# A retention block and a SwiGLU block on one core: the first head pair by chunks of 128 tokens, products of the identity around the first transposes, and another order of the first loads

## The chip, the cores and the metric

The kernel runs on one core of a Trainium2 chip. The metric is the device time of one execution in microseconds (us), the median of several runs. A core has five engines with a queue of instructions each: TensorE (PE in the profile; PEld is its weight load), VectorE (DVE), ScalarE (ACT), GpSimd (POOL) and SyncE (SP). Transfers (DMA) are issued from the queues of SP, ScalarE and POOL. Each engine works its own queue in order.

## The reference

```python
# q, k, v: batch 8, heads 8, 576 tokens, head size 64, float32
scores = (1 / sqrt(64)) * q @ k.T
gamma = 1 - 2 ** (-5 - arange(H))                 # one decay per head
Dmat = where(i >= j, gamma ** (i - j), 0)
attn = (scores * Dmat) @ v                        # causal, no softmax
x = attn.transpose(0, 2, 1, 3).reshape(4608, 512)
g = x @ w_gate                                    # 512 x 1536, float64 in memory
out = (g * sigmoid(g) * (x @ w_val)) @ w_out      # w_out: 1536 x 512
```

## The kernel before

*Two stages that overlap.* Retention makes `x`; the second stage turns tiles of `x` into rows of the result. Tile 0 has 512 tokens (`T0`) and is done with plain products (`up0`, `down0`); the later ones have 1024 and use fewer products of sums and differences (lines 1186 and 1381, most of PE's time). An order written out by hand fixes each engine's queue.

*Pairs.* The 64 head and batch combinations are worked in pairs of heads; pair `i` is batch `i // 4`, heads `2p` and `2p + 1`. Pairs 0 to 3 (`i < HP`) give tile 0 and have a path of their own. A pair is cut into chunks of 64 tokens (`L`). Its steps:
- `load(i)`: q, k and v, 128 KB a transfer for pairs 0 to 3. For pairs 1 to 3 q comes in another order, is scaled by POOL (`scale_run`, line 735) and then transposed. `kn` is k, token by token; `v` likewise.
- `transposes(i)`: PE turns q and k of 4 x 128 tokens by the identity (line 466); copies put them into `qT` and `kT`. Then k is scaled for the states (`keys`, line 505 or 507).
- `scores(i)`: 16 products of 64 x 64 (line 573), two PE instructions each, within a chunk. `new_states(i)`: what each chunk adds to the state (line 543). `masked(i)`: the decay mask `near` (line 580), then the running states: `copies` (584), `pairs` (596), `odd` (603), `evens` (608).
- `own_values(i)` (line 532) and `earlier_values(i)` (line 559) sum the output in `outer`; `to_x(i)` puts it into `x` (line 640, a copy for pairs 1 to 3; line 645 for pair 0, which still has to be scaled by `qry`).

*Weights.* They are float64 in memory and come in 18 blocks of 1024 KB: block 0 is 256 columns of the gate, block 1 the same of val, 2 and 3 the next 256, 4 and 5 those after them; the list `order` mixes the later ones with blocks of `w_out`. `load_w(m)` fetches block m: 0 to 3 in transfers of 256 KB on SP, 0 and 1 half by half, block 4 on SP, block 5 and later on ScalarE's queue. Three raw places are used in turn, so block m + 3 or m + 4 is fetched when block m has been split; block 3 goes to `x_odd`. `split(j)` (lines 389 and 390, ScalarE) and `rounding(j)` (406 and 407, VectorE) make float32 of half block j; `rounding(j)` calls `split(j + 1)` unless told not to. The order of halves is: block 0 and block 1, first halves; their second halves; then both halves of block 2, of block 3, and so on.

*Tile 0's products.* `up0(f, chunks)` (line 853, or 850 for some) makes 128 columns of gate and val from `x` of the pairs in `chunks`: one product for each pair. After the last pair ScalarE takes the Silu (856) and VectorE multiplies (857). `up0(f)` uses banks A and B for even f, C and E for odd f, so `up0(f + 2)` waits for that Silu and that product. `up0(0)` and `up0(1)` need the halves of blocks 0 and 1; `up0(2)` and `up0(3)` those of 2 and 3.

*The order at the start.* `tick(t, 0, HP)` runs for t = 0 to 5: transposes of pair t, scores and states of pair t - 1, values of pair t - 2. In t = 3 come `split(0)`, `rounding(0)`, after it `load(4)` and `rounding(1)`; in t = 4 `up0(0)` for the first two pairs, pair 3, the fetch of block 5 (`held`), `split(4)` and `up0(1)` for two pairs; in t = 5 pair 3's values and `rounding(4)`, `rounding(5)`. Then `up0(0)` and `up0(1)` for pairs 2 and 3, `load(5)`, and a list `plan` in which `rounding(6)`, pair 4's tick, `rounding(7)` to `rounding(9)`, `up0(2)`, `up0(3)` and so on follow.

*The queues of the first loads.* SP: 64 columns of the table `tab`, half of pairs 0 and 1, `load(2)`, the rest of the table (line 337), `load(3)`, then the weight blocks 0 to 3, `load(4)`, block 4, `load(5)`. ScalarE: the other half of pairs 0 and 1 with the values of pair 1, then the Silu of line 316, which loads a table.

## Time and profile before

| | |
|---|---|
| runs | 1017.63, 1017.77, 1018.7 us; median 1017.77 |
| profiled execution | 1019.25 us; its span, first to last instruction, 1017.5 us |
| busy in the span | PE 1001.9 us, DVE 713.2, POOL 564.4, ACT 285.5 |
| PE busy in 0 to 5, 5 to 10, 10 to 15, 15 to 20, 20 to 25, 25 to 30 us | 0.58, 3.94, 4.28, 4.73, 3.75, 4.73 us |
| PE busy in 55 to 60, 125 to 130 us | 3.88, 3.75 us |
| read and written | 194.38 MB, mean 191 GB/s; 251 GB/s in the first 80 us |

The page gives for each engine the busy time and, below, the busy share in 40 slices of the span (a digit is tenths). A line of the timeline has the start and the length of a group of like instructions, the engine, the line of the kernel, the operation with the tile it writes and those it reads, the number of instructions and, in brackets, how long the engine stood idle before and what ended that. A product of float32 operands is two PE instructions. Lines of "SPq" and "ACTq" are DMA issues on those queues. A line of the waits has the waiting engine and line, what ended the wait, the sum in us, how often, and the longest. A line of the windows has a stretch, its length, then busy us (and instructions) of PE, PEld, DVE, ACT and POOL, the granted clock, the DMA engines' busy share and GB/s.

### The profile page before, as it was taken

The numbers are of one execution on the slowest core, as the hardware profiler recorded it, in microseconds if no ns is written. First come the engines' busy times: TensorE is split into PE (matmuls) and PEld (weight loads), VectorE is DVE, ScalarE is ACT, GpSimd is POOL, SyncE is SP. The second block draws the span as 40 slices with busy tenths as digits, with TensorE's granted clock in tenths as the row PEclk, the third lists the DMA queues.
The fourth block names the chain that finished last, engine by engine and source line by source line (L and its number), as shares of the span: only waits on it lengthen the run. The fifth ranks groups of instructions, "written<-read, shape, count | busy, mean of one in ns | idle before, by whom it ended". The sixth has DMA issues, their size and how long they took to land.

```text
span 1017.5 us, 21317 instructions
## 1 busy us (share of the span) xinstructions
PE 1001.9 (98%) x8336; PEld 825.5 (81%) x8336; DVE 713.2 (70%) x1203; ACT 285.5 (28%) x636; POOL 564.4 (55%) x591
## 2 busy tenths in 40 slices
PE   6999999999999999999999999999999999999998
PEld 5644455888888888888888888888888888888887
DVE  4478889678785765967768678866575767566644
ACT  4465622132423312133322101233320012232110
POOL 3400339979575318575565248756672586566515
PEclk9999999999999999999999999999999999999999
DMA  9999887777587887657677777434454554445653
GB/s 241 253 253 241 218 241 253 203 236 218 126 252 192 232 205 215 191 167 197 184 202 204 183 186 202 165 127 165 165 176 142 149 192 146 144 155 181 185 156 100
DMA packets 278892, 194.38 MB, mean 191 GB/s; under 512 B 212552, under 2 KB 246088, under 8 KB 278792
## 3 DMA queue, kind: packets, MB, share of 16 engines
q1 hardware_dynamic: 251464, 94.70, 36.5%
q10 hardware_dynamic: 26688, 97.92, 29.1%
q8 instruction: 66, 1.08, 0.5%
q0 software_dynamic: 640, 0.39, 0.2%
q14 instruction: 34, 0.28, 0.1%
HBM read 154.04 MB, written 38.93 MB: 190 GB/s over the span
## 4 chain that ended last, share of the span: by engine, by line
PE 83%; DMA 5%; DVE 4%; SPq 3%; ACT 2%; POOL 2%; issue 1%; ACTq 1%; DVEq 0%; POOLq 0%
PE bankB L1186 11%; PE bankC L1186 11%; PE bankA L1186 11%; PE bankE L1186 11%; PE bankB L1381 7%; PE bankC L1381 7%; PE bankE L1381 6%; PE bankA L1381 6%; PE inner L1186 2%; PE outer L1186 2%; DMA qk<-in_q_dram 1%; POOL rest L1042 1%; PE outer L532 1%; PE outer L559 1%; PE inner L573 1%
## 5 line engine op out<-in xcount | busy, mean ns | idle before, releaser
L1042 POOL TENSOR_TENSOR rest<-rest 128x512 f32<-128x512 f32 (+1 forms) x141 | 150.3, 1077 | 160.8 <-DVE rest L1042 113.2
L1201 POOL TENSOR_TENSOR arena<-rest,io 128x256 f32<-128x256 f32 x168 | 123.8, 748 | 90.9 <-ACT io L1200 86.3
L1200 ACT ACTIVATE io<-rest 128x256 f32<-128x256 f32 x192 | 79.1, 417 | 202.1 <-DVE rest L1042 134.1
L1186 PE MATMUL bankB<-rest,arena 128*128 128x256 f32 x448 | 114.7, 380 | 0.1
L1042 DVE TENSOR_TENSOR rest<-bankB,rest 128x512 f32<-128x512 f32 x116 | 78.6, 686 | 42.0 <-PE bankB L1186 29.5
L1186 PE MATMUL bankC<-rest,arena 128*128 128x256 f32 x416 | 106.4, 380 | 0.1
L1186 PE MATMUL bankA<-rest,arena 128*128 128x256 f32 x412 | 104.8, 379 | 0.0
L1042 DVE TENSOR_TENSOR rest<-bankC,rest 128x512 f32<-128x512 f32 x110 | 74.6, 685 | 39.3 <-PE bankC L1186 25.3
L1042 DVE TENSOR_TENSOR rest<-bankA,rest 128x512 f32<-128x512 f32 x110 | 74.6, 686 | 37.5 <-PE bankA L1186 18.9
L1042 DVE TENSOR_TENSOR rest<-bankE,rest 128x512 f32<-128x512 f32 x106 | 71.9, 685 | 36.8 <-PE bankE L1186 17.6
L1186 PE MATMUL bankE<-rest,arena 128*128 128x256 f32 x372 | 94.9, 380 | 0.6 <-DVE rest L1042 0.6
L1186 PEld LDWEIGHTS bankB<-rest,arena 128*128 128x128 f32 x448 | 84.6, 190 | 12.5 <-DVE rest L1042 0.7
L1186 PEld LDWEIGHTS bankC<-rest,arena 128*128 128x128 f32 x416 | 78.5, 190 | 11.9 <-DVE rest L1042 1.3
L1186 PEld LDWEIGHTS bankA<-rest,arena 128*128 128x128 f32 x412 | 78.1, 190 | 10.9 <-DVE rest L1042 0.2
L1186 PEld LDWEIGHTS bankE<-rest,arena 128*128 128x128 f32 x372 | 70.3, 190 | 10.7 <-DVE rest L1042 1.2
L1042 POOL TENSOR_TENSOR arena<-arena 128x256 f32<-128x256 f32 (+1 forms) x76 | 70.0, 943 | 9.0 <-PE bankC L1186 7.6
L886 POOL TENSOR_TENSOR rest<-rest 128x512 f32<-128x512 f32 x21 | 29.1, 1408 | 77.5 <-DVE rest L407 60.5
L1381 PE MATMUL bankB<-arena 128*128 128x256 f32 x264 | 61.0, 381 | 0.0
L1381 PE MATMUL bankE<-arena 128*128 128x256 f32 x264 | 60.8, 380 | 0.0
L1381 PEld LDWEIGHTS bankE<-arena 128*128 128x128 f32 x264 | 50.0, 190 | 6.9
L1381 PEld LDWEIGHTS bankB<-arena 128*128 128x128 f32 x264 | 49.8, 190 | 6.9
L1381 PE MATMUL bankA<-arena 128*128 128x256 f32 x240 | 55.3, 380 | 0.0
(267 smaller groups left out, 1879.0 us busy)
## 6 DMA issues: line engine op xcount, KB each, us to landing
arena<-up ACTq DMA_DIRECT2D x63, 896.0 KB, 4.7
arena<-dn ACTq DMA_DIRECT2D x65, 384.0 KB, 3.1
arena<-dn SPq DMA_DIRECT2D x39, 384.0 KB, 3.3
out_dram<-rest SPq DMA_DIRECT2D x31, 256.0 KB, 3.4
qk<-in_q_dram SPq DMA_DIRECT2D x108, 72.0 KB, 3.2
qk<-in_k_dram SPq DMA_DIRECT2D x108, 72.0 KB, 3.3
dn<-rest SPq DMA_DIRECT2D x26, 256.0 KB, 3.0
up<-arena SPq DMA_DIRECT2D x13, 512.0 KB, 5.8
```

What stands on the lines that cost most here:

```text
L532: m = nc.tensor.matmul(value(i, hl, c), s["v"][rows, at], ret[rows, c % 2 if whole(i) else hl, c // 2], start=start, stop=start, skip_grou ...
L559: nc.tensor.matmul(xr[half[hl]] if c + 1 == NC else value(i, hl, c), state[half[hl], c, :], s["qT"][half[hl], ts(c, L)], start=False, stop ...
L573: nc.tensor.matmul(sc[chunk(i, hl, 2 * c + r)[0], r if whole(i) else hl, c], kT[half[hl], at], qT[half[hl], at], start=True, stop=True, sk ...
L886: eng.tensor_tensor(out=dst, in0=srcs[0], in1=srcs[1], op=ALU.add if op[0] == "add" else ALU.subtract)
L1042: eng.tensor_tensor(out=out, in0=a, in1=b, op=ALU.add if sign > 0 else ALU.subtract)
L1186: m = nc.tensor.matmul(b[:, g * TB : (g + 1) * TB], w[:, g], x, start=(opens and g == 0), stop=True, skip_group_check=True)
L1200: nc.scalar.activation(out=s, in_=src[:, 0:TB], func=AF.Silu)
L1201: (nc.vector if busy and o != 2 and qd + 1 < NQ else nc.gpsimd).tensor_tensor(out=hid[:, qd, 2 * H + h, 2 * T + t], in0=src[:, TB : 2 * TB ...
L1381: nc.tensor.matmul(b[:, m * TB : (m + 1) * TB], lhs[:, qd, ts(m, P)], w[:, qd], start=(opens and qd == 0 and m == 0), stop=(qd == NQ - 1), ...
```

## The change

Pair 0 is worked by chunks of 128 tokens with functions of its own. `first_scores` transposes q and k with products of the identity with itself into bankB before (six), between (two) and after (one) them; nobody reads those. VectorE scales q while it takes it from the bank (`first_qry`), so the output of pair 0 needs no scaling any more and ScalarE copies it (`first_out`). Scores are 128 x 128, with a mask of their own (`first_near`); `first_states` makes four states instead of eight. The table gets 132 columns more, all in its first part.

The loads move: q and k of pair 0, then the table's first part, q and k of pair 1, then v of both (v of pair 1 behind the Silu on ScalarE), `load(2)`. `load(3)` comes after the first halves of blocks 0 and 1, the rest of the table after block 2. The order of pairs 0 to 3 is written out, with `up0(0)` in pieces between the pairs (`parts` picks gate or val). From `for c in range(2, HP)` on the order is as before. Lines that only rename or drop code for pair 0 in `transposes`, `masked` and `tick` are left out below.

```diff
-             both(g[:, None] ** L), both(g[:, None] ** (2 * L)), pieces, runs, both(scale * g[:, None] ** at),
+             both(g[:, None] ** L), both(g[:, None] ** (2 * L)), pieces, runs, g[:2] ** -lane, g[:2] ** (2 * L - lane),
+             np.repeat(scale * g[:2, None] ** np.arange(2 * L), L, axis=0), both(scale * g[:, None] ** at),
...
-            for h in heads:
-                queues[i % 2].dma_start(out=blocks(t)[:, h % 2], in_=v[b, h, 0:CW].rearrange("(c p) d -> p c d", p=P))
+                if i == 0 and queue is nc.sync:
+                    nc.sync.dma_start(out=tab[:, 0:NCOL], in_=decays[:, 0:NCOL])
+            def values():
+                for h in heads:
+                    queues[i % 2].dma_start(out=blocks(t)[:, h % 2], in_=v[b, h, 0:CW].rearrange("(c p) d -> p c d", p=P))
+            loaded[i] = (qk, kn, t)
+            return values
...
-    NCOL = 6 * H + 4 * HP
-    nc.sync.dma_start(out=tab[:, 0:NCOL], in_=decays[:, 0:NCOL])
-    load(0)
-    load(1)
+    NCOL = 6 * H + 4 * HP + 4 + P
+    values = [load(0), load(1)]
     ident = const.tile([P, P], F32, name="ident")
     make_identity(nc, ident)
     nc.scalar.activation(out=io[:, 0:1], in_=ident[:, 0:1], func=AF.Silu)
+    for f in values:
+        f()
+    load(2)()
...
+    first_inv, first_key, first_qry = tab[:, NCOL - P - 4 : NCOL - P - 2], tab[:, NCOL - P - 2 : NCOL - P], tab[:, NCOL - P : NCOL]
...
+    first_near, first_ret = arena[:, 2048:2304], arena[:, 1024:2048].rearrange("p (h c i) -> p h c i", h=2, i=P)
+    nc.gpsimd.affine_select(out=first_near.rearrange("p (h i) -> p h i", i=P), in_=first_inv.unsqueeze(2).to_broadcast([P, 2, P]),
+                            compare_op=ALU.is_ge, fill=0.0, base=0, channel_multiplier=-1, pattern=[[0, 2], [1, P]])
...
-    load(2)
-    nc.sync.dma_start(out=tab[:, NCOL:], in_=decays[:, NCOL:])
-    load(3)
...
-    for f in range(2):
-        for m in range(2):
-            load_w(m, (f,))
+    for m in range(2):
+        load_w(m, (0,))
+    load(3)()
+    for m in range(2):
+        load_w(m, (1,))
     load_w(2)
+    nc.sync.dma_start(out=tab[:, NCOL:], in_=decays[:, NCOL:])
     load_w(3)
...
+            for n, (t, src, bank) in enumerate(((kT, kn, bankC), (qT, qk, bankE))):
                 for c in range(NFULL):
-                    to = bank[:, c : 4 * P : NFULL] if t is qT and scaled(i) else bank[:, ts(c, P)]
-                    nc.tensor.transpose(to, src[:, ts(c, P)], ident)
-
-            def put(t, _, bank):
-                if i or t is qT:
-                    copy(t[:, 0:CW], bank)
-                else:
-                    copy(t[:, 0 : CW // 2], bank[:, 0 : CW // 2])
-                    nc.scalar.copy(t[:, CW // 2 : CW], bank[:, CW // 2 :])
-
-            if i + 1 == HP:
-                for part in parts:
-                    turn(*part)
-                pieces = [lambda part=part: put(*part) for part in parts]
-            else:
-                for part in parts:
-                    turn(*part)
-                    put(*part)
+                    nc.tensor.transpose(bank[:, c : 4 * P : NFULL] if n else bank[:, ts(c, P)], src[:, ts(c, P)], ident)
+                pieces.append(lambda t=t, bank=bank: nc.scalar.copy(t[:, 0:CW], bank))
...
-        return [keys] + pieces
+        return pieces + [keys] if i < HP else [keys] + pieces
...
+    first = [(c, hl) for c in range(NFULL) for hl in range(2)]
+    head = lambda c, hl: slice((2 * c + hl) * D, (2 * c + hl + 1) * D)
+    sums = bankA[:, 0 : NFULL * D].rearrange("p (c d) -> p c d", d=D)
+    def first_scores():
+        qk, kn, vt = loaded.pop(0)
+        qT = early[0]
+        st[0] = dict(qT=qT, kn=kn, v=vt)
+        for src, bank, idle in ((None, None, 6), (qk, bankE, 2), (kn, bankC, 1)):
+            for c in range(NFULL if bank else 0):
+                nc.tensor.transpose(bank[:, ts(c, P)], src[:, ts(c, P)], ident)
+            for _ in range(idle):
+                nc.tensor.matmul(bankB[:, 0:P], ident, ident, start=True, stop=True)
+        blocks = lambda a: a.rearrange("p (c i) -> p c i", i=P)
+        table = lambda a: a.unsqueeze(1).to_broadcast([P, NFULL, P])
+        nc.vector.tensor_tensor(out=blocks(qT), in0=blocks(bankE), in1=table(first_qry), op=ALU.mult)
+        nc.vector.tensor_copy(kT[:, 0 : CW // 2], bankC[:, 0 : CW // 2])
+        nc.scalar.copy(kT[:, CW // 2 : CW], bankC[:, CW // 2 :])
+        for hl in range(2):
+            at = kn[:, 0:CW].rearrange("p (g d) -> p g d", d=D)[:, hl::2]
+            nc.vector.tensor_scalar(out=at, in0=at, scalar1=first_key[:, hl : hl + 1], scalar2=None, op0=ALU.mult)
+        for c, hl in first:
+            nc.tensor.matmul(inner[:, hl, ts(c, P)], kT[half[hl], ts(c, P)], qT[half[hl], ts(c, P)],
+                             start=True, stop=True, skip_group_check=True)
+        for hl in range(2):
+            nc.vector.tensor_tensor(out=first_ret[:, hl], in0=blocks(inner[:, hl]), in1=table(first_near[:, ts(hl, P)]), op=ALU.mult)
+    def first_states():
+        s = st[0]
+        for c, hl in first:
+            nc.tensor.matmul(sums[half[hl], c], s["kn"][:, head(c, hl)], s["v"][:, head(c, hl)],
+                             start=True, stop=True, skip_group_check=True)
+        nc.vector.tensor_copy(state[:, 1], sums[:, 0])
+        for c in range(1, NFULL):
+            nc.vector.scalar_tensor_tensor(out=state[:, c + 1] if c + 1 < NFULL else end_states[:, 0], in0=state[:, c],
+                                           scalar=step[:, HP : HP + 1], in1=sums[:, c], op0=ALU.mult, op1=ALU.add)
+    def first_own():
+        for c, hl in first:
+            st[0]["own"] = nc.tensor.matmul(outer[half[hl], 0, ts(c, P)], st[0]["v"][:, head(c, hl)], first_ret[:, hl, c],
+                                            start=(c == 0), stop=(c == 0), skip_group_check=True)
+    def first_out():
+        s = st.pop(0)
+        wait = nc.tensor.nop()
+        tc.add_manual_dep(wait.ins, s["own"].ins.name,
+                          mybir.DependencyInfo(mybir.DependencyClass.Sync, mybir.DependencyReason.DATA), reason="row halves")
+        for c, hl in first[2:]:
+            nc.tensor.matmul(outer[half[hl], 0, ts(c, P)], state[half[hl], c], s["qT"][half[hl], ts(c, P)],
+                             start=False, stop=True, skip_group_check=True)
+        nc.scalar.copy(out=xs[0][:, 0], in_=outer[:, 0])
+    def new_pair(i):
+        scores(i, True)
+        new_states(i)
+        pieces.extend(masked(i))
+        go_on(3)
+    def turn_pair(i):
+        for f in transposes(i):
+            f()
...
-    def up0(f, chunks):
+    def up0(f, chunks, parts=range(2)):
 
         pair = banks[2 * (f % 2) : 2 * (f % 2) + 2]
-        for gv, bank in enumerate(pair):
+        for gv in parts:
+            bank = pair[gv]
             for c in chunks:
...
-    for t in range(HP + 2):
-        tick(t, 0, HP)
-
-        if t == 3:
-            load(HP)
-        for j in {3: (1,), 5: (4, 5)}.get(t, ()):
-            rounding(j)
+    scale_run(1)
+    first_scores()
+    scale_run(2)
+    turn_pair(1)
+    first_states()
+    first_own()
+    new_pair(1)
+    turn_pair(2)
+    first_out()
+    split(0)
+    rounding(0, False)
+    scale_run(3)
+    new_pair(2)
+    own_values(1)
+    split(1)
+    up0(0, [0], [0])
+    earlier_values(1)
+    to_x(1)[0]()
+    put = transposes(3)
+    rounding(1, False)
+    for f in put:
+        f()
+    load(HP)
+    up0(0, [1], [0])
+    up0(0, [0], [1])
+    split(2)
+    own_values(2)
+    earlier_values(2)
+    up0(0, [1], [1])
+    to_x(2)[0]()
+    rounding(2)
+    rounding(3, False)
+    new_pair(3)
+    while held:
+        held.pop()()
+    split(4)
+    up0(1, range(2))
+    own_values(3)
+    earlier_values(3)
+    to_x(3)[0]()
+    for j in (4, 5):
+        rounding(j)
```

## The prediction

> **What bounds the kernel now.** I read the page first: PE 1001.9 of 1017.5 us, so nearly every PE gap and every slow PE stretch is paid, and the change can only act through them. The waits then say where the 15.6 us of gaps lie. From 58 us to the end the largest is 1.3 us, at 127 us; all the rest that matters is in the first 58 us, which is where the change works.
>
> ```profile
> PE   6999999999999999999999999999999999999998
> PE bankE L864 <- DVE arena L857: 1.3, 1, 1.3
> PE bankA L853 <- ACT io L856: 1.1, 1, 1.1
> ```
>
> Second, the timeline of the start. The same four transposes or 32 small products take some 0.6 of the time from 16 us on, with no other change:
>
> ```profile
> 5.87 1.09 PE L466 MATMUL bankB<-ident,kn 128*128 128x128 f32 x4 [0.36 <-DMA kn<-in_k_dram]
> 12.33 1.13 PE L573 MATMUL inner<-rest,kT 64*64 64x64 f32 x32 [0.72 <-ACT rest L470]
> 15.10 1.11 PE L466 MATMUL bankB<-ident,rest 128*128 128x128 f32 x4
> 16.01 0.64 PE L466 MATMUL bankA<-ident,rest 128*128 128x128 f32 x4
> 17.43 0.69 PE L573 MATMUL inner<-rest,kT 64*64 64x64 f32 x32 [0.17 <-ACT rest L470]
> ```
>
> (The granted-clock column says 1.00 throughout; only durations show it.) From the start of L573 to the start of its successor it is 0.81 us at 7.47 and 0.46 at 17.43: a ratio of 1.76. PE became fast after its first stretch without a gap, 12.33 to about 15.9 us. Third, the timeline from 24 to 58 us:
>
> ```profile
> 30.87 1.88 PE L853 MATMUL bankE<-rest,arena 128*128 128x512 f32 x4
> 30.97 0.44 ACTq L370 DMA_DIRECT2D rest<-in_moe_w_val_dram  x1
> 43.95 0.81 SPq L370 DMA_DIRECT2D rest<-in_moe_w_gate_dram  x1
> 52.80 0.67 ACT L389 ACTIVATE rest<-rest 128x512 f32<-128x512 f32 x1 [6.18 <-DMA rest<-in_moe_w_gate_dram]
> 56.77 0.59 ACT L856 ACTIVATE io<-bankA 128x512 f32<-128x512 f32 x1
> 57.41 3.70 PE L853 MATMUL bankA<-rest,arena 128*128 128x512 f32 x8 [1.12 <-ACT io L856]
> ```
>
> Here PE, which has been continuous since 34 us, stops at 56.29 and resumes at 57.41. It waits for `up0(2)`'s Silu to free bankA. That Silu stands on ScalarE behind `split`s of weight block 4, and ScalarE stood idle 6.18 us until that block (1024 KB, issued by SP at 43.95) landed at 52.70. So block 4 at 52.70 + 4.71 us fixes the start of `up0(4)`, however early PE comes to it. Last, windows of 1 us: how full the DMA engines are before that landing (last two columns: share, GB/s).
>
> ```profile
> 25.00:26.00 1.00, 1.00 (x4) 0.39 (x3) 0.56 (x2) 1.00 (x3) 0.00 (x0) 1.00 0.94 260
> 28.00:29.00 1.00, 0.73 (x37) 0.57 (x28) 0.69 (x1) 0.01 (x1) 0.00 (x0) 1.00 0.69 200
> 29.00:30.00 1.00, 1.00 (x8) 0.49 (x3) 0.42 (x1) 0.37 (x1) 0.00 (x0) 1.00 0.61 161
> ```
>
> From 2 us on they are full; 28 to 30 us is the largest hole.
>
> **Part 1: the start, up to the end of `up0(1, range(2))`.** Before, that ends at 32.75 us.
>
> *Identity products.* Each is two PE instructions of 128 columns. A 256-column instruction takes 0.216 us (L1186, 8 in 1.73 us), so 128 columns take 0.108, or 0.19 while slow (by 1.76): nine cost 1.9 to 3.4 us. Six fill the idle time between the identity (ready at 1.50) and the first q (4.42 before); six by 0.38 slow end at 3.8. Two (0.76) meet the 0.36 us wait for k, one (0.38) the 0.52 us wait for `kT`. If PE stays slow they overrun by about 0.4 us.
>
> *Scores of pair 0.* The 32 instructions of 64x64 (0.69 fast, 1.13 slow) become 16 of 128 columns on half the rows. No row has that shape: below, half of 0.69 is 0.35; above, 16 x 0.108 = 1.7 one after another; I take pairs side by side as the small ones run, 0.86 fast and 1.5 slow. States stay near 0.4, own values grow by the same 0.4, earlier values to some 0.6. Together PE gets 0 to 2 us more, I take 1.1.
>
> *VectorE.* q's scaling takes the copy's place (0.69 for 0.69). The mask becomes two of 0.69, one more; against it `pairs` (0.47) and `evens` (0.48) fall away for a 64-column copy (0.2), and the three L645 outputs (1.30) move to one ScalarE copy of 0.59. About 1 us less. POOL gets one `affine_select` more (128x256; two of 64x512 take 1.37), before `scale_run(1)` and under the wait for q of pair 1.
>
> *Transfers.* The table's part needed first grows from 64 to 196 columns, all of it by 132: 0.068 MB. Landings fit a line: k of pair 1 (1.60 MB issued up to it) at 9.64, `x_odd` (7.63 MB) at 30.89, so 3.52 us a MB. `load(3)` (0.79 MB) and the table's remainder (0.26) now stand behind weight halves: the first halves of blocks 0 and 1 land near 16.4 for 19.8 us, pair 3's v at 19.1 (16.1), the second halves at 22.8 (23.5), blocks 2 and 3 at 26.5 and 31.1 (27.2, 30.89). Queued behind the later pair 3 on SP are only those halves. Values of pair 1 now stand behind the Silu on ScalarE (table load 1.28), harmless: they are first read near 12 us.
>
> *Sum.* PE's work is spread over transfers, so the last transfer sets the end: second halves 22.8 + `split` 1.23 (ScalarE, 21.23 to 22.46) + rounding 1.26 (VectorE, 22.02 to 23.28) = 25.3, + 1.88 for the val half of `up0(1)` = 27.2 us, against 32.75: **5.5 us ahead**. Pair 0's shape, the filled gaps and the faster clock lie under the transfers.
>
> **Part 2: from there to `up0(4)`.** Own and earlier values of pair 3 and 16 products follow (32.68 to 41.14). Half of the products need pair 3's copies, which stand on ScalarE behind the issue of block 5 (30.97 before, just after `x_odd` landed at 30.89) and one `split`; that can give back up to 1.7 us. `up0(2)` thus starts at 35.7 to 37.4. Its 13.9 us with `up0(3)` end at 49.6 to 51.3 (the last quarter needs VectorE's rounding that ended at 46.82; it wants it at 46.1 to 47.8). With 1.3 us of pair 4, PE stands before `up0(4)` at 50.9 to 52.6, 3.7 to 5.4 us earlier. The wait of 1.12 us becomes 4.8 to 6.5: the stall is moved, not removed, unless block 4 lands earlier.
>
> **Part 3: block 4's landing.** The same megabytes go ahead of it (pairs 0 to 4, blocks 0 to 3, and on ScalarE's queue 5 and 6) plus 0.068 MB: +0.24 us. Block 5 may now be issued while `x_odd` is still moving and fill the hole of 28 to 30 us: shares 0.69 and 0.61 against 1.06 (mean of 23 to 28) lack 0.8 us; I take 0.7. Bounds: nothing is filled, +0.24; everything under 1.06 from 28 to 52 us is filled, 2.8, so -2.5 us. [...]
>
> **Part 4: after `up0(4)`.** ScalarE's splits and the later weight loads hang on the same landing, so VectorE's late product at 127 us moves with it. Total: +0.24 - 0.7 = **-0.5 us**. The profiled execution (1019.25 us, span 1017.5) becomes 1018.75; it lies 1.48 us over the median of 1017.77, so I predict 1017.3.
>
> **Rivals.**
> A, *block 4 comes much earlier*. Blocks 5 and 6 (30.97 and 36.58 before) are issued up to 5 us earlier, and two busy queues move more: in 5 to 12 us, with both, shares are 1.17 to 1.36. That over 28 to 52 us would give the 2.5 us of the bound, or up to the 5.4 us PE is ahead: 1012.4 to 1015.3, about 1014.8. Against: 43 to 52 us holds little but block 4 itself.
> B, *the clock falls back in the longer wait* before `up0(4)`. No wait in this trace after 16 us exceeds 1.3 us, so nothing shows it; for it speaks that the start stayed slow until 15.9 us, though PE had worked 11.5 us with gaps of 0.2 to 0.7. It decides if the wait passes the length the clock tolerates. Price: the one gapless slow stretch lasted 3.5 us, and by the ratio 1.76 that loses 1.5; 11.5 us would lose 5.0. With -0.5 that is +1.0 to +4.5, from 1018.8 to 1022.3, some of it hidden by the 1.3 us at 127. [...]
> C, *SP is blocked ahead of block 4*. One SP issue of v stood 7.9 us until a w_out block of ScalarE's queue landed:
>
> ```profile
> SPq L287 <- DMA rest<-in_moe_w_out_dram: 7.9, 1, 7.9
> ```
>
> If block 5, issued earlier, comes to hold up pair 4's loads so, block 4 is issued late. Block 5 needs some 8 us; what moves meanwhile is one queue's at half the rate, so 2 to 4 us are lost: 1020 to 1021.5. Against: before 44 us SP never waited over 1.4 us.
> D, *the products don't raise the clock* (transposes lie between). Pairs 0 and 1 then cost PE what they cost before (7.47 to 15.1 us hold 7 us, 3 of them by the slow rate); PE is at most those 3 us less ahead, still ahead of block 4: 1017.5.
>
> **Chances.** Forecast 0.36 and D 0.02: within 0.2% (2 us, about what a measurement of this kernel tells from no change). A 0.26: faster. B 0.20: 0.07 within, 0.13 slower. C 0.16: slower. So faster 0.26, same 0.45, slower 0.29. The forecast's own range is 1015.3 to 1018.5; with most of A, B and C it is 1013.7 to 1020.9.
>
> **What will show it.** Right: transposes and products at the fast durations before 10 us; `up0(1)`'s val half done near 27 us; ScalarE's long wait for block 4 again ending at 52 to 53; PE's wait before `up0(4)` at 4 to 6 us. Wrong: block 4 landing under 50 us (A); L853 of 128x512 at 0.76 us each instead of 0.43 after that wait (B); an SP wait of several us between 29 and 44 (C); slow transposes after 10 us (D). A `up0(4)` that starts by more than 2 us off 57 us breaks the forecast.

## The result, and the profile after

The changed kernel takes 1022.64 us (median of 6 runs, 1021.35 to 1026.0) against 1017.7 for the one before in the same session: a ratio of 1.0062, 95% interval 1.0049 to 1.0075. It is slower by 4.9 us; 1017.3 was forecast, with a range of 1015.3 to 1018.5. The profiled execution took 1022.28 us, its span is 1020.6 us (1017.5 before).

The page of the changed kernel: busy time with the number of PE instructions (46 products and 46 loads fewer than the 8336 before, which is 23 products of the program, each two loads and two products), the busy shares of PE, and the queue that brings the instructions themselves.

```profile
PE 1005.3 (99%) x8290; PEld 828.6 (81%) x8290; DVE 708.8 (69%) x1200; ACT 286.8 (28%) x636; POOL 564.4 (55%) x592
...
PE   8989999999999999999999999999999999999998
...
q8 instruction: 66, 1.08, 0.4%
```

PE is busy 3.4 us *longer* than before although it has fewer instructions: some of them ran slowly. The list of PE's waits has the rest; the columns are the sum, how often, and the longest.

```profile
PE bankA L868 <- ACT io L871: 2.9, 1, 2.9
PE inner L559 <- issue: 2.0, 1, 2.0
PE bankA L879 <- issue: 1.6, 1, 1.6
...
PE bankA L868 <- DVE arena L416: 1.3, 1, 1.3
```

The first is the wait ahead of `up0(4)`, 1.1 us before. The second and the third were not there before. "Issue" means that PE waited for nothing that the profile shows. (All lines of the changed kernel lie 15 further down from `up0` on: 868 and 871 are 853 and 856 of before, 398 and 416 are 389 and 407, 559 and 529 are 573 and 543, 518 and 545 are 532 and 559.)

The start, in the timeline of PE: the transposes run at the fast rate from the second four on, and the val half of `up0(1)` for two pairs (the L868 into bankE) ends at 30.1 us.

```profile
4.28 1.06 PE L734 MATMUL bankE<-ident,qk 128*128 128x128 f32 x4
5.75 0.60 PE L734 MATMUL bankC<-ident,kn 128*128 128x128 f32 x4
28.26 1.88 PE L868 MATMUL bankE<-rest,arena 128*128 128x512 f32 x4
```

The place where the forecast ended, ScalarE's and PE's timelines merged: block 4 lands, its `split`s, the Silu, then `up0(4)`.

```profile
51.92 0.66 ACT L398 ACTIVATE rest<-rest 128x512 f32<-128x512 f32 x1 [3.28 <-DMA rest<-in_moe_w_gate_dram]
53.06 0.64 PE L559 MATMUL inner<-qT,kT 64*64 64x64 f32 x30
55.93 0.58 ACT L871 ACTIVATE io<-bankA 128x512 f32<-128x512 f32 x1
56.57 5.40 PE L868 MATMUL bankA<-rest,arena 128*128 128x512 f32 x8 [2.87 <-ACT io L871]
61.80 2.74 PE L868 MATMUL bankB<-rest,arena 128*128 128x512 f32 x6
```

`up0(4)` starts 0.84 us earlier than before, but its gate half takes 5.40 us instead of 3.70, so its val half starts 0.85 us *later* (61.80 for 60.95). Windows show why (the clock fell at 56.69 and at 623.30 us; the bounds lie 0.05 us behind that); after the stretch and its length come busy us (and instructions) of PE, PEld, DVE, ACT and POOL, then the granted clock.

```profile
49.90:53.30 3.40, 3.40 (x63) 1.69 (x63) 0.52 (x2) 1.38 (x3) 0.00 (x0) 1.00 1.15 202
53.30:56.74 3.44, 0.57 (x27) 0.44 (x20) 1.82 (x4) 2.93 (x6) 0.00 (x0) 0.99 0.71 143
56.74:60.15 3.41, 3.41 (x5) 1.35 (x6) 2.80 (x6) 2.89 (x6) 0.00 (x0) 0.51 1.09 344
60.15:63.60 3.45, 3.45 (x10) 1.54 (x9) 3.31 (x10) 2.08 (x4) 0.00 (x0) 1.00 1.12 344
619.94:623.35 3.41, 1.45 (x43) 1.25 (x38) 0.00 (x0) 0.40 (x2) 3.33 (x6) 0.99 0.84 247
623.35:626.76 3.41, 3.41 (x10) 2.70 (x9) 2.25 (x6) 0.77 (x2) 0.28 (x1) 0.51 0.54 183
```

Behind each of the two long waits stands one stretch of 3.41 us at half the clock, and then the full clock again. Each loses half its length, 1.7 us. The second wait lies inside pair scores at 620 us, where before had none:

```profile
619.96 0.46 PE L559 MATMUL inner<-qT,kT 64*64 64x64 f32 x15
622.38 0.46 PE L559 MATMUL inner<-qT,kT 64*64 64x64 f32 x15 [1.96 <-issue]
622.77 1.59 PE L1201 MATMUL bankC<-rest,arena 128*128 128x256 f32 x4
```

PE stops in the middle of 32 like instructions whose operands had long been there. The trace has a transfer of 16 KB on q8, the instruction queue, starting at 619.88, and one at 123.02, just ahead of the 1.58 us before `down0` (L879).

Followed through the run, the changed kernel is 0.9 us behind from 74 to 410 us, 0.2 from 422 us (before waited 0.6 us for VectorE at 412), 0.8 us *ahead* from 540 to 620 us, 3.1 behind after it and 3.05 at the end. What it gained between 520 and 540 us is no wait of the list: in the profile of before PE took 0.9 us longer for the same instructions there, in short pauses, and nothing here says why.

### The profile page after: what moved, and what is told of

Read it like the earlier page. It is cut to its first block, busy times and chain, and to the rows that moved or that the text cites. A ratio compares the mean times of both kernels' runs of the same rounds, so it can differ in the third digit from the quotient of the medians.

```text
span 1020.6 us, 21221 instructions
## 1 busy us (share of the span) xinstructions
PE 1005.3 (99%) x8290; PEld 828.6 (81%) x8290; DVE 708.8 (69%) x1200; ACT 286.8 (28%) x636; POOL 564.4 (55%) x592
## 4 chain that ended last, share of the span: by engine, by line
PE 94%; DMA 2%; DVE 1%; SPq 1%; issue 1%; ACT 0%; ACTq 0%; DVEq 0%
PE bankB L1201 12%; PE bankC L1201 12%; PE bankA L1201 11%; PE bankE L1201 11%; PE bankB L1396 7%; PE bankC L1396 7%; PE bankE L1396 7%; PE bankA L1396 6%; PE bankA L868 2%; PE outer L518 2%; PE bankC L868 2%; PE bankB L868 2%; PE inner L1201 2%; PE outer L1201 2%; PE bankE L868 2%; PE outer L545 2%
## 5 line engine op out<-in xcount | busy, mean ns | idle before, releaser
L1201 PEld LDWEIGHTS bankE<-rest,arena 128*128 128x128 f32 x372 | 70.6, 191 | 10.5 <-DVE rest L1057 0.6
L1396 PE MATMUL bankC<-arena 128*128 128x256 f32 x240 | 55.4, 380 | 0.0
L1396 PEld LDWEIGHTS bankB<-arena 128*128 128x128 f32 x264 | 49.8, 190 | 6.9
```

What stands on the lines that cost most here:

```text
L1201: m = nc.tensor.matmul(b[:, g * TB : (g + 1) * TB], w[:, g], x, start=(opens and g == 0), stop=True, skip_group_check=True)
L1396: nc.tensor.matmul(b[:, m * TB : (m + 1) * TB], lhs[:, qd, ts(m, P)], w[:, qd], start=(opens and qd == 0 and m == 0), stop=(qd == NQ - 1), ...
```

## The experiments

All compare with the kernel before on the same chip; 1.0062 is the mark to hold them against. Unless a line says otherwise the edit is made to the changed kernel.

**Bringing PE's instructions back to their place.** The theory: PE's instructions arrive in transfers of 16 KB (the 66 on q8 above), and where one is wanted in a burst of small products, PE runs dry; 23 products fewer move every such point. The first test adds instructions without work: six more banks of `up0` are taken as 256 columns twice, 96 PE instructions more.

```diff
-                if f == 2 or f == 3 and gv == 0:
+                if 4 <= 2 * f + gv < 13:
```

> The changed kernel with six more of up0's banks made by 8 products of 256 columns for 4 of 512, as three are already: the same PE time, 96 PE instructions more, so that from 80 us on the stream stands where it stood before the change, but for 4. Theory 2: the stalls of 1.6 us at 124 and 2.0 us at 620 us go, and the slow stretch behind the latter; the wait and the slow stretch at 57 us stay: some 1018 to 1020 us. Rival (start alone): the stall at 620 us stays, 1022 to 1023 us.

Measured: 1021.44 us, ratio 1.0057 (1.0040 to 1.0075). The stalls at 124 and 620 us are gone, and the clock stays full behind 62 us; a new one of 1.70 us ("issue") stands at 75.7 us, and the wait ahead of `up0(4)` is 2.6 us with half rate behind it. The stalls moved as the theory says; the time, between the two expectations, hardly did.

The same edit on the kernel *before*, ten banks (160 instructions more; the changed kernel has 66 transfers for 16580 recorded instructions, 251 each, so 160 more is nearly the same place in them as 92 fewer, 252 apart):

```diff
-                if f == 2 or f == 3 and gv == 0:
+                if 4 <= 2 * f + gv < 17:
```

> [...] Nothing of the change itself. Theory 2: a PE stall of some 2 us at 620 us and a slow stretch behind it, 1019.5 to 1022 us. Rival (start alone): as before, 1017 to 1018 us.

Measured: 1018.91 us, ratio 1.0032 (1.0015 to 1.0050), between the two expectations and 3.2 us slower than before. With nothing of the change in it, the timeline has the changed kernel's stall, in the same burst, one instruction further on, but no half rate behind it:

```profile
616.32 0.51 PE L573 MATMUL inner<-qT,kT 64*64 64x64 f32 x16
619.49 0.45 PE L573 MATMUL inner<-qT,kT 64*64 64x64 f32 x14 [2.66 <-issue]
```

Next, 92 empty instructions ahead of `up0(4)`:

```diff
+        if f == 4:
+            plan.append(lambda: [nc.tensor.nop() for _ in range(92)])
```

> After, with 92 empty PE instructions (no operation) ahead of up0(4), where PE waits anyway. They put every later PE instruction at the place in PE's instruction stream that it has in the kernel before (23 products fewer are 92 instructions fewer). Theory (the two late stalls come from the place in the stream): the stalls of 1.58 us at 124 us and of 1.96 us at 620 us vanish, and with the second the 3.41 us at half rate behind it (1.7 us); VectorE's wait near 126 us (1.25 before) may return. The wait of 2.9 us ahead of up0(4) and the half rate behind it stay. Span 1020.6 - 1.96 - 1.7 - 0.3 = 1016.6 to 1017.2 us, ratio to before 1.001 to 1.003. Rival (the late stalls come from the new timing of the transfers or of VectorE, not from the stream): both stalls stay, span 1020 to 1021, ratio 1.005 to 1.007.

Measured: 1024.05 us, ratio 1.0069 (1.0054 to 1.0084). Both stalls are there (2.1 and 1.96 us). It proves nothing against the theory: the empty instructions have no records, and the 16 KB transfers come at the same PE products as in the changed kernel, so they took no place in PE's stream. The run serves as the changed kernel once more.

So real instructions, 23 small products that nobody reads, where PE would wait anyway:

```diff
+    def extra_products(full, small):
+        for n in [P] * full + [L] * small:
+            nc.tensor.matmul(outer[0:n, 1, 384 : 384 + n], ident[0:n, 0:n], ident[0:n, 0:n], start=True, stop=True, skip_group_check=True)
...
+            if f == 3:
+                plan.append(lambda: extra_products(0, 23))
             plan.append(lambda t=tick_at[f]: tick(t, HP, FIRST))
```

> After, with 23 small products (64x64 of the identity with itself, 92 PE instructions, 46 of them products that cost 0.69/32 = 0.02 us each, 1.0 us) ahead of pair 4's scores, where PE waits later anyway. Every PE instruction from there on has the place in PE's stream that it has in the kernel before. Theory (place in the stream): no stall near 124 us (1.6 to 2.1 in after and its repetition) and none near 620 us (1.96 in both), no half rate behind 620 us; VectorE's waits near 126 us (1.25) and 412 us (0.6) return as in before. The wait ahead of up0(4) is 1.9 to 2.2 us, so the half rate behind it stays in about half of the runs. Span 1020.6 - 1.96 - 1.7 - 0.4 + 0.6 = 1017.1, ratio to before 1.001 to 1.004. Rival (timing of transfers, not the stream): both stalls stay, ratio 1.005 to 1.007.

Measured: 1021.66 us, ratio 1.0055 (1.0035 to 1.0076). The 32 instructions at 621 us run through, and near 128 us PE waits for VectorE as it did before. In the timeline:

```profile
621.59 0.64 PE L559 MATMUL inner<-qT,kT 64*64 64x64 f32 x30
```

and in the list of its waits:

```profile
PE bankE L879 <- DVE arena L872: 1.4, 1, 1.4
```

And the kernel before with 41 such products ahead of pair 4's scores, 164 instructions more, 256 apart from the 92 fewer of the changed kernel:

> [...] Theory (place in the stream): a stall of 1.5 to 2.7 us appears near 620 us and one of 1 to 2 us near 124 us in place of VectorE's 1.25; half rate behind the former where it falls so. With 0.6 us for the small products that the wait of 1.1 us ahead of up0(4) does not hide: span 1017.5 + 0.6 + 2.0 + 0.5 - 0.6 = 1020, with half rate 1021.7; ratio 1.002 to 1.005. Rival (the stalls belong to the change's own timing): no stall at 620 us, ratio 0.999 to 1.001.

Measured: 1026.14 us, ratio 1.0094 (1.0074 to 1.0115). At 620 us stands the changed kernel's stall in the kernel before:

```profile
625.26 0.41 PE L573 MATMUL inner<-qT,kT 64*64 64x64 f32 x14
627.62 0.46 PE L573 MATMUL inner<-qT,kT 64*64 64x64 f32 x16 [1.95 <-issue]
```

At 124 us no stall came, against the expectation. And the products took 4.9 us, not the 1.8 behind the 0.6 us of that sum: all of them use one corner of the array and write one place, and they cost 0.06 us an instruction, where the price had taken over 0.02 from pair scores. So its total says nothing; the stall does.

Over all 20 profiles the stall near 620 us (1.4 to 2.7 us) stands in every one of the eight whose instruction count puts them there (the changed kernel, five variants that leave its count, and the two of before moved to it), and in none of the other twelve. In the six of the changed kernel's count PE stops with 6151 or 6152 matmul instructions behind it, in the two of before with 6278, which is 126 or 127 further on: 252 to 254 instructions with the weight load that each has, where a transfer stands for 251 recorded ones. That the place in the stream makes this stall is settled. What it is worth is not: put into the kernel before it cost 3.2 us, but the kernel with 23 small products, which has lost it, still takes 0.55% more than before, and its gain over the changed kernel lies within the intervals.

**The clock behind the wait ahead of `up0(4)`.** First, seven identity products directly ahead of `up0(4)`, alone:

```diff
+    def warm():
+        for _ in range(7):
+            nc.tensor.matmul(outer[:, 1, 384:512], ident, ident, start=True, stop=True, skip_group_check=True)
...
+        if f == 4:
+            plan.append(warm)
```

> The changed kernel with seven more products of the identity with itself (28 PE instructions, some 2.7 us), not read, ahead of up0(4), in PE's wait of 2.87 us. Theory 1 (the longer wait lets PE's clock fall): up0(4)'s first bank takes 3.6 us and not 5.4, no slow stretch at 57 to 60 us, PE 1.7 us earlier from there on. Theory 2 (what is lost later, 1.96 us of PE stall at 620 us, hangs on the place of the pairs' small products in PE's instruction stream, which the change made 92 instructions shorter): the stream is moved by 28 more, so that stall may go or move to another pair. Rival (the loss comes from the new order of loads and work at the start alone): neither changes anything, 1022 to 1023 us.

Measured: 1026.68 us, 1.0103 (1.0089 to 1.0117): badly placed. `outer` was still to be read by VectorE, so PE stood 7.03 us instead of 2.9, with two half-rate stretches behind it. With four banks split as well it was the same (1.0098). Then 13 products ahead of pair 4's scores, where nothing holds them up (the 40 empty instructions again took no place):

```diff
+            if f == 3:
+                plan.append(lambda: [nc.tensor.matmul(outer[:, 1, 384:512], ident, ident, start=True, stop=True, skip_group_check=True)
+                                     for _ in range(13)] + [nc.tensor.nop() for _ in range(40)])
```

> After, with 13 more products of the identity with itself (52 PE instructions, 13 x 0.216 = 2.8 us) and 40 empty PE instructions ahead of pair 4's scores, behind up0(3), where nothing holds them up: the wait ahead of up0(4) is filled with useless work and not shortened, and the stream is at the place of before. Theory (the half rate comes from PE standing idle): up0(4) starts at 56 to 57 us as in after, with a wait under 0.3 us, and its gate half takes 3.7 us; no stall at 620 us. Span 1020.6 - 1.7 - 3.7 = 1015.2 us, ratio 0.999 to 1.001. Rival (up0(4) is slow for its operands, or for transfers that run at the time): the gate half still takes 5.4 us, ratio 1.001 to 1.003.

Measured: 1025.38 us, 1.0080 (1.0061 to 1.0100). The timeline and the windows show the gap filled, and `up0(4)`, at almost the same time as in the repetition (58.0 against 58.6), at full rate:

```profile
53.76 3.06 PE L1518 MATMUL outer<-ident 128*128 128x128 f32 x26
58.00 3.70 PE L868 MATMUL bankA<-rest,arena 128*128 128x512 f32 x8
```

```profile
56.70:60.10 3.40, 3.40 (x75) 2.19 (x74) 2.06 (x4) 2.89 (x6) 0.00 (x0) 1.00 0.90 273
```

3.70 us instead of 5.40: idle PE costs the clock, not the operands or the transfers of that time. But a stall of 2.83 us ("issue") appeared at 76 us, and the whole gained nothing. Five large and 18 small products shorten the wait instead ("the one before" in the expectation is the kernel with 23 small products):

> As the one before, with 5 products of 128x128 and 18 of 64x64 (again 92 PE instructions, 1.1 + 0.8 = 1.9 us): the wait ahead of up0(4) falls to about 1.0 to 1.3 us. Theory (PE's clock halves for 3.41 us when it stands idle for about 1.7 us or more of a stretch of that length): no half rate behind it, up0(4)'s gate half at 3.7 us; and no late stalls. Span 1.0 to 1.7 us less than the one before, 1015.5 to 1016.5, ratio 0.999 to 1.002. Rival: as for the one before, 1.005 to 1.007.

Measured: 1021.07 us, 1.0047 (1.0031 to 1.0062). The wait is 0.9 us, the gate half 3.70, no stall at 620 us: all as expected up to 100 us. Then PE waits 3.1 us for a Silu at 105 us, with half rate behind it, as the last `split`s ahead of that Silu began at 102.0 us only, when ScalarE had waited 5.3 us for a rounding of VectorE; in the changed kernel their like began at 100.0 us.

**The Silu ahead of the splits.** The wait ends with a Silu that stands behind block 4's splits on ScalarE. Put ahead of them:

```diff
-            plan.extend(lambda j=j: rounding(j) for j in (2 * m, 2 * m + 1))
+            plan.extend(lambda j=j: rounding(j, j != 7) for j in (2 * m, 2 * m + 1))
...
-    plan.insert(1, lambda: tick(HP, HP, FIRST))
+    plan.append(lambda: tick(HP, HP, FIRST))
+    plan += [lambda: up0(2, range(HP)), lambda: split(8)]
```

> After, with ScalarE's Silu of up0(2) put ahead of the splits of weight block 4, and both halves of block 3 rounded before pair 4's tick. Theory (the wait ahead of up0(4) is the Silu's place behind block 4 on ScalarE, and the half rate follows from the length of that wait): up0(4) then waits only for block 4's first half to be split and rounded, 51.9 + 0.66 + 0.6 + 0.43 + 0.69 = 54.3 to 54.8 us instead of 56.57; the wait shrinks from 2.87 to about 0.8 us, no half rate follows, up0(4)'s gate half takes 3.7 us instead of 5.4. Span 1020.6 - 2.0 - 1.7 = 1016.9 us if the stalls at 124 and 620 us stay (the stream of PE is not changed), ratio 1.001 to 1.003. Rival 1 (block 4's landing moves later by the other order, or the next wait, near 60 to 75 us, takes the gain back): under 1 us gained, ratio 1.005 or more. Rival 2 (up0(4) is slow for a reason other than the wait ahead of it, for example its operands): the gate half still takes 5.4 us after the shorter wait.

Measured: 1024.25 us, 1.0064 (1.0048 to 1.0080). At its place it does what was expected:

```profile
55.91 3.70 PE L868 MATMUL bankA<-rest,arena 128*128 128x512 f32 x8 [0.51 <-DVE arena L416]
104.64 1.12 PE L868 MATMUL bankA<-rest,arena 128*128 128x512 f32 x2 [1.34 <-ACT io L871]
```

But PE now waits for a Silu at 103 us, and the stalls at 123 (2.1) and 622 us (1.4) stay, the former now with half rate behind it. Nothing is gained in sum. The same with 92 empty instructions, which means the same kernel again:

> After with both edits: the Silu of up0(2) ahead of block 4's splits, and the 92 empty PE instructions ahead of up0(4). If both theories hold the gains add: 1020.6 - 3.7 - 3.7 to 4.0 = 1012.9 to 1013.5 us of span, ratio 0.997 to 0.999, faster than before. If only the stream's theory holds 1017, if only the wait's 1017, if neither 1020.6.

Measured: 1023.36 us, 1.0054 (1.0036 to 1.0072): no wait ahead of `up0(4)` (55.24), 3.3 us at 104 us, 2.2 at 128, 1.9 at 625.

**The nine products.** Left out, with nine small ones later to keep the place of the others:

```diff
-            for _ in range(idle):
-                nc.tensor.matmul(bankB[:, 0:P], ident, ident, start=True, stop=True)
```

> After without the nine products around the first transposes; 9 small products (36 PE instructions, 0.4 us) ahead of pair 4's scores keep the later stream of after. Theory (block 4's landing sets up0(4), what happens on PE before lies under it): PE is slow up to 12 to 17 us, up0(4) starts within 1 us of after's 56.6 to 58.6, both late stalls stay; ratio 1.005 to 1.008 as for after. Rival (the nine products carry the change, without them PE falls behind the transfers): up0(4) starts 2 us later or more, ratio 1.009 or more. Other rival (the nine products themselves cause the loss, by the early clock): the late stalls go, ratio under 1.003.

Measured: 1025.16 us, 1.0088 (1.0072 to 1.0104), between the first two expectations. `up0(4)` starts at 56.87 us, within 0.3 us of the changed kernel; the late stalls stay, and 3.4 us at 104 us come on top. So the nine products are neither what costs the time nor what `up0(4)` hangs on; whether they are worth 0.2% stays open.

**The order of the transfers.** Block 4 had landed at 51.9 to 54.9 us in the eleven profiles with the new order (mean 53.2) and at 49.8 to 52.8 in the three with the old one. SP's queue shows a difference ahead of it. The eight issues of pair 4's q and k, which stand before block 4, took 9.3 us in the profile of before and 11.9 in that of the changed kernel, which began them earlier (two lines each):

```profile
29.37 3.55 SPq L282 DMA_DIRECT2D qk<-in_q_dram  x4
32.96 5.75 SPq L282 DMA_DIRECT2D qk<-in_k_dram  x4
```

```profile
27.54 6.19 SPq L290 DMA_DIRECT2D qk<-in_q_dram  x4
33.77 5.69 SPq L290 DMA_DIRECT2D qk<-in_k_dram  x4
```

They took 10.5 to 12.6 us in all eleven profiles with the new order, and block 4 was issued at 41.0 to 44.9 us there. In the kernel before, its edits and the two below with the old order they took 7.1 to 9.3, and block 4 was issued at 38.9 to 40.0, but for the first profile of before (43.95). What makes the issues longer no run shows.

Now the kernel before, profiled once more:

> The kernel before, unchanged, for a second profile of it: a span of 1013 to 1016 us (the profile shown at the beginning has 1017.5, most other executions 1013 to 1015), weight block 4 landing at 49.5 to 51.5 us instead of 52.7, PE without a wait or with under 0.5 us ahead of up0(4), no stall near 620 us.

Measured: 1018.71 us, span 1017.0. The span misses the expectation by 1 us. Block 4 came at 51.67, 0.2 us after the latest expected, and PE did not wait for it, as expected; but PE was late itself, by a wait of 3 us at 21 us and half rate behind it:

```profile
24.32 0.69 PE L532 MATMUL outer<-ret,v 64*64 64x64 f32 x32 [2.98 <-ACT rest L390]
51.67 0.67 ACT L389 ACTIVATE rest<-rest 128x512 f32<-128x512 f32 x1 [5.43 <-DMA rest<-in_moe_w_gate_dram]
59.40 1.98 PE L853 MATMUL bankA<-rest,arena 128*128 128x512 f32 x4
```

Then the changed kernel with pair 3 and the table ahead of the weights again:

```diff
     load(2)()
+    nc.sync.dma_start(out=tab[:, NCOL:], in_=decays[:, NCOL:])
+    load(3)()
```

> After, with pair 3's loads and the table's remainder ahead of the weight halves again, as in before; everything else as in after. Theory (the order of transfers makes block 4 late): block 4 lands at 49.5 to 52 us, 2 us earlier than the mean of 53.2; PE's wait ahead of up0(4) falls from 2.9 or 3.2 us to about 1; the stall near 620 us with its half rate stays. 1022.6 - 2 - 1 = 1019 to 1020, ratio to before 1.002 to 1.004. Rival (block 4 is late for another part of the change): ratio as for after, 1.005 to 1.007, block 4 at 52 to 55 us.

Measured: 1024.65 us, 1.0079 (1.0063 to 1.0095), a ratio above even the rival's, though the theory's mechanism is there: block 4 does land 3.7 us earlier than that mean, at 49.48, and PE does not wait for it. But now PE waits 6.1 us for block 0 (L418 is the rounding here), has half rate from 18.3 to 28.5 us, and comes to `up0(4)` at 60.5:

```profile
22.69 2.08 PE L868 MATMUL bankA<-rest,arena 128*128 128x512 f32 x2 [6.08 <-DVE arena L418]
49.48 0.68 ACT L400 ACTIVATE rest<-rest 128x512 f32<-128x512 f32 x1 [2.12 <-DMA rest<-in_moe_w_gate_dram]
```

With six more banks split, as in the first experiment:

> The one before, with six more banks of up0 taken by 256 columns (96 PE instructions more, no more PE time), which brings the later PE instructions within 4 of their place in before. Theory: both parts of the loss are undone, no stall near 620 us: ratio 0.998 to 1.001. Rival: the order is not the rest: 1.003 to 1.005.

Measured: 1021.41 us, 1.0060 (1.0040 to 1.0080), above both expectations: no stall at 620 us, but one of 3.6 at 76.5 us. And the kernel before with pair 3 behind the first halves:

```diff
     for f in range(2):
         for m in range(2):
             load_w(m, (f,))
+        if f == 0:
+            load(3)
```

> Before, with only the loads of pair 3 moved behind the first halves of weight blocks 0 and 1, as in after; no PE instruction changes. Theory (the order of transfers makes block 4 late): block 4 lands 1 to 2 us later than in before, up0(4) starts 1 us later, ratio 1.001 to 1.002. Rival: the order does nothing, 0.9995 to 1.0005, or a gain by earlier weights, under 0.9995.

Measured: 1021.23 us, 1.0045 (1.0032 to 1.0059): slower than either expectation, yet not through block 4 (51.7 us); PE lost 3.7 us in three waits at 17 to 22 us and had half rate from 22.3, and ScalarE's first split began at 26.3 us instead of 21.2.

**Both causes at once.** Block 4 issued ahead of pair 4's loads, both halves of block 3 rounded before pair 4's tick, PE's instructions at exactly the place of before:

```diff
-        for src, bank, idle in ((None, None, 6), (qk, bankE, 2), (kn, bankC, 1)):
+        for src, bank, idle in ((None, None, 5), (qk, bankE, 2), (kn, bankC, 1)):
...
-                if f == 2 or f == 3 and gv == 0:
+                if 4 <= 2 * f + gv < 13:
...
-    load(HP)
     up0(0, [1], [0])
     up0(0, [0], [1])
     split(2)
+    load(HP)
...
-    plan.insert(1, lambda: tick(HP, HP, FIRST))
+    plan.append(lambda: tick(HP, HP, FIRST))
```

> After, with weight block 4 issued ahead of pair 4's loads on SP, both halves of block 3 rounded before pair 4's transposes, and PE's later instructions at exactly their place in before (six more banks by 256 columns, +96, and one identity product less, -4). Theory (up0(4) waits for block 4 alone, and the late stalls are the stream's): block 4 lands under 42 us, up0(4) starts when PE comes to it, at 53.5 to 55.5 us, span = that + 957.5 + 0.2 to 2.5 = 1012 to 1015.5, ratio to before 0.997 to 1.000. Rival (pair 4's loads, now behind block 4, take its place: PE waits for pair 4's keys ahead of up0(4)): a wait of 2 to 5 us with half rate behind it, span 1016 to 1019, ratio 1.001 to 1.004.

Measured: 1025.14 us, 1.0069 (1.0052 to 1.0086). Neither expectation. The wait went 14 us back, ahead of `up0(2)`: ScalarE stood 6.6 us until 41.1 before it could issue block 6, while pair 4's q was coming, and the Silu of `up0(0)` is behind that issue. And a stall of 5.0 us is at 78 us (the timeline, then the list of PE's waits).

```profile
41.63 0.66 ACT L398 ACTIVATE rest<-x_odd 128x512 f32<-128x512 f32 x1 [6.55 <-DMA qk<-in_q_dram]
43.51 6.51 PE L865 MATMUL bankA<-rest,arena 128*128 128x256 f32 x16 [3.67 <-ACT io L871]
```

```profile
PE outer L689 <- issue: 5.0, 1, 5.0
```

With pair 4's scores behind `up0(4)` (`tick_at` with 4: 5 for 3: 5, the later loads kept near their places):

> As the one before, with pair 4's scores and pair 5's tick behind up0(4) instead of ahead of it, so that pair 4's loads have 7 us more. Theory: PE comes to up0(4) at 52 to 54 us without a wait; span that + 959 (pair 4's 1.3 us now lie behind) + 0.2 to 2.5 = 1011 to 1015, ratio 0.996 to 0.999. Rival (the transfers as a whole are late, so the wait only moves to a later block or pair): waits of PE between 60 and 110 us of 2 to 5 us in all, ratio 1.000 to 1.004.

Measured: 1024.52 us, 1.0069 (1.0056 to 1.0083): 3.4 us ahead of `up0(2)` again, 3.5 us at 75 us. No version beats the kernel before.

## The account by terms

What holds the twenty profiles together is a sum. Take the start of `up0(4)` from PE's timeline, add PE's waits of over 0.2 us behind it and half the length of each half-rate stretch behind it: the rest of the span is nearly the same everywhere.

| kernel (profile) | span | `up0(4)` | waits after | half rate / 2 | rest |
|---|---|---|---|---|---|
| before | 1017.5 | 57.4 | 2.1 | 0 | 958.0 |
| before, again | 1017.0 | 59.4 | 0.2 | 0 | 957.3 |
| before, 160 instructions more | 1016.1 | 55.9 | 2.9 | 0 | 957.2 |
| changed | 1020.6 | 56.6 | 3.8 | 3.4 | 956.8 |
| changed, again (the empty instructions) | 1023.2 | 58.6 | 4.3 | 3.4 | 956.9 |
| Silu first | 1020.6 | 55.9 | 5.6 | 1.7 | 957.4 |
| 13 products in the wait | 1020.5 | 58.0 | 4.7 | 0 | 957.8 |
| stream back, 23 small | 1018.5 | 58.6 | 2.6 | 0 | 957.4 |
| stream back, 5 + 18 | 1020.6 | 58.1 | 3.9 | 1.7 | 957.0 |
| old order | 1022.9 | 60.5 | 3.4 | 1.7 | 957.3 |
| block 4 first | 1026.2 | 61.5 | 5.8 | 1.7 | 957.1 |

The rests shown agree within 1.2 us. Of the nine left out eight have rests of 957.0 to 958.2; the ninth, the last experiment, has 959.6, as pair 4's scores lie behind `up0(4)` there. In the two profiles each, `up0(4)` starts at 58.4 us in the mean before and at 57.6 in the changed kernel: no loss there, and a gain of 0.8 that is not clear of chance, as two profiles of one kernel lie 2 us apart. Waits and half rate behind it take 7.5 us in the mean where before has 1.2. In the two profiles shown first the parts add up so: -0.8 for the start of `up0(4)`, +1.7 for waits, +3.4 for half rate, -1.2 for the rest, 3.1 us in all.

The runs without a profile agree as far as they go. Each lists its mean granted clock, and 1 less that, times the span, is what half rate lost: 2.9 us in the twelve runs of the changed kernel and its repetition (0.9972) against some 0.7 (0.9993 in the runs of before beside the repetition). That is 2.2 us; the stall at 620 us is 1.96, and the one near 125 us 1.6 to 2.1 where before had nothing to 1.25. Together 4.5 to 6.3, for 4.9 and 6.3 measured, if the stalls are in every run as they are in the two profiles, which the runs do not show.

## Why the prediction was wrong

*Part 1, the first weights, was right, its sum was not.* ScalarE waited for the first halves and split them from 15.8 and 17.6 us; 16.4 had been forecast as the landing of both, and in before the first split began at 21.2. PE ran fast from 5.5 us on (rival D is out). But `up0(1)` for two pairs ended at 30.1 us, 2.6 us ahead instead of 5.5. What failed is "the last transfer sets the end". From 17.87 us, when the first rounding let it go, PE worked 12.2 us with 0.3 of gaps, and in that queue pair 3's scores (25.35) stood ahead of *both* halves of `up0(1)`, 1.82 and 1.88 us, which began at 26.4. The last rounding did come late, at 27.4 for 25.3, but PE was not waiting for it. So PE's own work set the end, not what it waited for, and the faster clock and pair 0's shape did not lie under the transfers.

*Part 2 was right in kind.* PE came to `up0(4)` at 53.70, 1.1 us later than the later end of the forecast, for that same reason, and waited 2.87 us (4.8 to 6.5 forecast).

*Part 3 was right for this execution.* Block 4 came 0.9 us earlier, `up0(4)` 0.84 (0.5 forecast). But the premise under it, that block 4 sets `up0(4)` in the kernel before, rested on one execution. In the four other profiles of before or of before with small edits, block 4 came at 49.8 to 51.7 us and PE did not wait there at all. Over all profiles block 4 came later with the new order (53.2 in the mean) than in the kernel before (52.8 and 51.7), not 0.5 us earlier: the sign that came true is luck.

*Part 4 is the step that failed.* It let everything behind `up0(4)` move with block 4's landing, so that the total was the landing's -0.5 us, and put what comes behind at nothing else, without a row for it. There were 1.7 us of half rate, 1.58 and 1.96 us of stall and another 1.7 of half rate. Only VectorE's product at 127 us was named, and it was covered by the stall beside it.

*Rival B was the better forecast*: its place, its sign and its price of 1.5 us for one slow stretch (1.7 measured) came true; it had a chance of 0.20. Its 1018.8 is near what is left when the late stalls are taken off (1022.6 - 1.6 - 2.0 - 1.7 + 1.25 for VectorE's wait = 1018.6), but that close only by luck, as the rest of the span alone differs by 1.2 us between the two profiles. A wait forecast at 4.8 to 6.5 us, where none over 1.3 had been seen at full rate, deserved the larger chance. The slow stretch behind the wait of 2.87 us lasted 3.41 us (the windows above). Rival A is out (block 4 at 51.92). Rival C's wait was not there, SP never waited over 1.7 us between 29 and 44 us, but its effect was in part: SP's issues of pair 4 took longer (above) and block 4 was issued at 44.78 for 43.95. The half rate of one queue in its price no run shows: in the kernel before SP's queue alone moved 277 GB/s from 12 to 28 us and ScalarE's alone 334 from 58 to 62, with 251 as the mean of the first 80. The last two kernels show a relative of it on ScalarE's queue.

*What no rival had* is PE's instruction stream. In the two profiles of the changed kernel it carries 2 us of the loss by the stall at 620 us and 1.7 by the clock behind it, and it has nothing to do with what the change computes. No version of the changed kernel got that time back in its median, as other waits came in its place; so the parts are measured in the profiles, and what each is worth in the 4.9 us is not shown.

What stays open: why the transfers of the first 120 us differ by some 2 us between executions of one kernel, why repairs of the first wait bring another at 40 or at 104 us, and when a transfer of instructions starts. The stalls of 1.7 to 5.0 us at 75 to 78 us in five variants, whose counts differ by the end (+4, 0 and -40 against before), tell something of the last: in all five PE stops with 851 or 852 matmul instructions behind it and goes on 2.5 to 3.1 us after a transfer of 16 KB has started. The kernel before and the two kernels with 23 products pass that place without a stall, and there the same transfer, the sixth, had started 5.2 to 8.0 us ahead. So in these profiles where PE stopped went with the place, and whether it did with the start of the transfer; what starts it late no run shows.

## What to carry to other kernels

A wait in one profile of a kernel is one draw: before it is made the premise of a forecast, it should be found in a second execution. Where one engine is busy 98% of the span, split the span into the start of its steady part, a constant, its waits and its slow stretches, and ask of a change what it does to each, the waits far behind the edit among them: 160 instructions more early on were enough to put a stop of 2.66 us near 620 us into the kernel before. And a wait that is moved together into one piece can cost more than its length: 2.87 us ahead of `up0(4)` had half rate behind them that cost 1.7 more.

## What the runs showed of the hardware

*PE's granted clock changed in fixed steps.* In each trace its changes lie on a grid of 3.413 us, wherever the waits are (in the changed kernel half rate is recorded for 3.413 us from 56.69 and from 623.30, which are 166 steps apart). Over the 20 profiles, the ends of the spans left out, a step at full rate in which PE stood idle for 2.0 us or more was followed by a step at half rate in all 13 cases; with 1.65 to 1.99 us idle in 16 of 21; with less, never. So a wait of 1.9 us was dear or not by where it fell: 1.96 us within one step at 620 us cost 1.7 more, 2.66 us across two steps in the kernel before with 160 instructions more cost nothing more.

*PE stopped behind the start of an instruction transfer.* The transfers of 16 KB on the instruction queue, 66 in the run, take 0.9 to 1.9 us in the kernel before and 0.9 to 1.6 in the changed one. Where one starts within the burst of a pair's small products at 620 us, PE stopped for 1.4 to 2.7 us, at the same instruction within two, and went on 2.5 to 2.7 us after its start. The kernel before with 160 and with 164 instructions more stopped there as the changed kernel with 92 fewer does, 252 and 256 apart, beside 251 recorded instructions to a transfer. Of the changed kernel's 66 transfers two had such a stop behind them, 1.58 and 1.96 us.

*A small product has no single price.* 46 instructions of 64x64 on one corner of the array and into one place took 2.8 us, 0.06 us each; pair scores, which alternate between corners and write different places, take 0.69 us for 32, 0.02 each. No run tells the corner from the place.
